# Pooled attention and a multiplicative feed-forward on one core: the last two chunks of 512 tokens by one level of Strassen's scheme

## The chip, the cores and the metric

The kernel runs on one core of a Trainium2 chip. The metric is the device time of one execution in microseconds (us). Before the change three runs took 415.0, 415.41 and 415.67 us; the median is 415.41. One execution was also taken by the profiler.

Names of engines in the profile: PE is the matrix unit (PEld its weight loads), DVE the vector engine, ACT the scalar engine, POOL GpSimd, SP the engine that issues most DMAs. A queue is marked with a q, as in SPq.

## What is computed

Shapes: q, k, v are 8 x 8 x 1152 x 64 (batch, heads, sequence, head size) in fp32; 4608 tokens of 512 come out.

```python
q_pool = q.reshape(B, H, S // 2, 2, D).mean(axis=3)
attn = softmax(q_pool @ k.T / sqrt(D))              # 576 x 1152 for each batch and head
x = (attn @ v).transpose(0, 2, 1, 3).reshape(4608, 512)
h = ((x @ w1) * (x @ w2)) @ w3                      # w1, w2: 512 x 1024, w3: 1024 x 1024
out = h @ w_out                                     # w_out: 1024 x 512
```

## The kernel before, in words

Two heads of one batch are a pair; there are 32 pairs. For each pair the scores, transposed, come off PE in steps of 512 columns for both heads (`scores`, L422), ACT takes the exponential into a large ring of f16 in SBUF (`ring`, L436), and PE multiplies the ring's columns with v (`av_mm`, L449). A unit of this product is 128 pooled tokens of one pair, or 64 of two; there are 144. DVE normalizes (`av_norm`, L479) and the result goes, transposed, to `xT` (512 features on partitions, 4 blocks of 128; 5 x 576 tokens of room). For the first pairs and for the units of 64, PE turns it and DVE copies it (L515, L517), for the others SP's DMA does (`x_dma`, L469).

The feed-forward part works on chunks of 512 tokens, numbers 0 to 8 (`moe_groups`, L582). `T` (`T16`, 1024 x 512 in f16) is w3 times w_out and is made once, early in the run, in groups of eight 256-column matmuls (L544). Per chunk there are 16 projection groups of four 512-column matmuls, w1 and w2 in turn (`proj`, L563, L566): the first result is copied to SBUF as `asb`, the second is multiplied with it into `gT` (gate, L599). Then four groups of eight 512-column matmuls with T (L610) give 128 tokens of output each; they are scaled, copied to `osb` and stored.

A planner (`_visits`, L191) fixes in advance, with costs of its own, in which visit which attention unit and which feed-forward group stands in PE's queue. A chunk is put in the list `loose` under the unit after which its x is there. PSUM has eight banks: one for the product with v and the turns (`avb`), one for groups (`mo`), and three pairs for scores and groups (`psc`, named `mot` for groups). Each engine works through its instructions in the order in which they are written; `manual_schedule` leaves that order alone.

When all units are done (`tail[0]`, L806) only feed-forward groups are left. Then ACT copies `asb` (L593) and shares the scaling (L616 DVE, L617 ACT), and the stores go through SP instead of POOL's queue (L618; L621 before). The last group is cut in 384 and 128 columns (`go_last`, L623) and the last two stores go through ACT's queue. In between, a flag is worked out from the softmax sums: DVE compares (L816 to L824), one small matmul sums over the partitions (L827), and all engines load the flag (L833). If it were set, a slower general path would run behind (`_general`, L24); with these inputs it is not.

POOL casts and adds inputs (`cast_kq`, `cast_v`), issues the early loads, and issues the stores of all chunks but the last ones. SP issues the later loads, the transposes of k and q (L363) and of x (L473).

Of the kernel before, what the change touches and what calls it, by code (L numbers as in the profile page):

```python
# [253 lines left out]

@with_exitstack
def kernel(
# [26 lines left out]
    QM = 4  # L283
# [16 lines left out]
    ps = fast.enter_context(tc.tile_pool(name="ps", bufs=1, space=bass.MemoryType.PSUM))  # L300
# [12 lines left out]
    wosb = msb.tile([128, NF, dm], FP16)  # L313
# [207 lines left out]

    def bank(scored):
        if tail[0] or scored:
            return ps.tile([128, 2, 512], FP32, tag="psc", bufs=3, name="mot")[:, 0, :]
        return ps.tile([128, 512], FP32, tag="mo", bufs=1, name="mo")
# [43 lines left out]
    def store(eng, pos, osb):  # L569
        b, r = pos // (2 * Sq) * 2, pos % (2 * Sq)  # L570
        if r == QM * 128:
            for u in range(2):
                r0 = (b + u) * Sq + QM * 128
                eng.dma_start(out=out[r0:r0 + QT, :], in_=osb[u * QT:u * QT + QT, :])
            return
        if r > QM * 128:
            b, r = b + 1, r - QM * 128 - 2 * QT
        eng.dma_start(out=out[b * Sq:b * Sq + QM * 128, :].rearrange("(p c) n -> p c n", c=QM)[:, r // 128, :], in_=osb)  # L578

    final, near = [], [False]  # L580

    def moe_groups(c):  # L582
# [20 lines left out]
        tts = list(range(0, CH, 128))  # L603
        if c in final:
            tts.sort(key=lambda tt: (c * CH + tt) % (2 * Sq) != QM * 128)
        for n, tt in enumerate(tts):
            def go(po, tt=tt, n=n):
                near[0] = c in final and n >= len(tts) - 3
                for ft in range(NF):
                    nc.tensor.matmul(po, t["g"][:, ft, tt:tt + 128], T16[:, ft, :],  # L610
                                     start=(ft == 0), stop=(ft == NF - 1))

            def put(po, tt=tt):
                osb = msb.tile([128, dm], FP32, tag="osb", bufs=3)
                if tail[0]:
                    nc.vector.tensor_scalar_mul(out=osb[:, 0:256], in0=po[:, 0:256], scalar1=1.0 / (SCL * SCL))  # L616
                    nc.scalar.mul(out=osb[:, 256:512], in_=po[:, 256:512], mul=1.0 / (SCL * SCL))  # L617
                    store(nc.scalar if c in final and tt == tts[-2] else nc.sync, c * CH + tt, osb)  # L618
                else:
                    nc.vector.tensor_scalar_mul(out=osb, in0=po, scalar1=1.0 / (SCL * SCL))  # L620
                    store(nc.gpsimd, c * CH + tt, osb)  # L621

            def go_last(po, tt=tt):  # L623
                osb = msb.tile([128, dm], FP32, tag="osb", bufs=3)
                for hs in (slice(0, 384), slice(384, dm)):
                    ph = ps.tile([128, 2, 512], FP32, tag="psc", bufs=3, name="mol")[:, 0, 0:hs.stop - hs.start]
                    for ft in range(NF):
                        nc.tensor.matmul(ph, t["g"][:, ft, tt:tt + 128], T16[:, ft, hs],
                                         start=(ft == 0), stop=(ft == NF - 1))
                    if hs.start:  # L630
                        nc.scalar.mul(out=osb[:, hs], in_=ph, mul=1.0 / (SCL * SCL))
                    else:
                        nc.vector.tensor_scalar_mul(out=osb[:, hs], in0=ph, scalar1=1.0 / (SCL * SCL))
                store(nc.scalar, c * CH + tt, osb)

            if c in final and n == len(tts) - 1:
                yield 2, go_last, None, 0.0
            else:
                yield 2, go, put, 0.0
# [83 lines left out]
    for c in range(B * Sq // CH):  # L723
        n = 0
        for b in range(B):
            for t in range(NT5):
                if xpos(b, t) < (c + 1) * CH and xpos(b, t) + (128 if t < QM else QT) > c * CH:
                    p = b * HP + HP - 1
                    i = unit_of(p, t)
                    n = max(n, i + 2, index[(p, QM - 1)] + 1 + HELD if p >= XD and t < QM else 0)  # L730
        loose.setdefault(min(n, NU + 1), []).append(c)
    final.extend(loose[max(loose)])
# [40 lines left out]
    for vis in range(NVIS):  # L773
        if vis == T_START:
            queue.append(t_groups())
        for s in range(vis * VS, vis * VS + VS):
            pn = (s * G + G - 1) // FLAT
            if pn != seen:
# [6 lines left out]
                if 0 < pn < NP - 2:  # L785
                    prepare(pn + 2)
                elif pn + 2 == NP:
                    cast_v(NP - 1)
            scores(s)
# [21 lines left out]
    release()  # L811

# [12 lines left out]
    for _ in range(12):  # L825
        fill()
    nc.tensor.matmul(avb[0:1, 0:1], okh, ones, start=True, stop=True)  # L827
    badi = const.tile([1, 1], mybir.dt.int32)
    nc.vector.tensor_scalar(out=badi, in0=avb[0:1, 0:1], scalar1=-1.0, scalar2=float(128 * NQ),
                            op0=ALU.mult, op1=ALU.add)  # L830
    while not near[0]:
        fill()
    bad = nc.values_load(badi[0:1, 0:1], min_val=0, max_val=128 * NQ)  # L833
    while fill():
        pass
    fast.close()
# [32 lines left out]
```

## Time and profile before

| | |
|---|---|
| median of 3 runs | 415.41 us |
| span of the profiled execution, first to last instruction (the profile gives no other time of it) | 414.1 us |
| PE busy, from 328 to 358, 358 to 368, 367.5 to 388.2 and 388.2 to 409.4 us | 30.00, 10.00, 20.70, 21.14 us |
| DVE busy in the same stretches | 17.35, 6.09, 7.28, 7.64 us |
| ACT busy in the same stretches | 19.11, 0.38, 6.21, 6.20 us |
| POOL busy in the same stretches | 3.06, 1.09, 0, 0 us |
| mean granted clock of PE | 0.999 |
| last exponential ends | 349.08 us |
| last matmul ends, last store is issued | 409.34 us, 409.69 us |

How to read the rows of the profile. The page's strips cut the span in 40 equal slices and give the busy share of each in tenths. A row of a group names line, engine, operation, output and inputs with shapes and types, the count, then busy time and mean duration, then the idle time before it and what ended it. A row of the timeline has start, duration, engine, line, operation, and in brackets the idle time before it. In the chain of waits each piece is what the end of the run was waiting for at that time.

### The profile page before, as it was taken

The numbers are of one execution on the slowest core, as the hardware profiler recorded it, in microseconds if no ns is written. First come the engines' busy times: TensorE is split into PE (matmuls) and PEld (weight loads), VectorE is DVE, ScalarE is ACT, GpSimd is POOL, SyncE is SP. The second block draws the span as 40 slices with busy tenths as digits, with TensorE's granted clock in tenths as the row PEclk, the third lists the DMA queues.
The fourth block names the chain that finished last, engine by engine and source line by source line (L and its number), as shares of the span: only waits on it lengthen the run. The fifth ranks groups of instructions, "written<-read, shape, count | busy, mean of one in ns | idle before, by whom it ended". The sixth has DMA issues, their size and how long they took to land.

```text
span 414.1 us, 12744 instructions
## 1 busy us (share of the span) xinstructions
PE 399.9 (97%) x5337; PEld 246.9 (60%) x5337; DVE 205.5 (50%) x573; ACT 323.4 (78%) x353; POOL 167.6 (40%) x212
## 2 busy tenths in 40 slices
PE   3899999999999999999999999999999999999995
PEld 1477787565556655566556556655777655644442
DVE  1256665665356535554455436553556346744241
ACT  4878979898989998899999999999899986022321
POOL 4979976470655316504535155505532210010000
PEclk9999999999999999999999999999999999999999
DMA  8999999999799898959999999998975440030302
GB/s 263 210 320 289 269 286 312 348 247 265 185 238 252 221 286 278 242 70 278 273 264 280 264 252 270 292 260 163 303 207 121 85 90 15 16 114 2 101 0 108
DMA packets 90832, 86.34 MB, mean 209 GB/s; under 512 B 59664, under 2 KB 64272, under 8 KB 90768
## 3 DMA queue, kind: packets, MB, share of 16 engines
q1 hardware_dynamic: 81312, 58.80, 59.1%
q0 software_dynamic: 8880, 25.63, 21.6%
q10 hardware_dynamic: 576, 1.05, 0.8%
q8 instruction: 42, 0.69, 0.7%
q14 instruction: 22, 0.18, 0.1%
HBM read 67.11 MB, written 9.44 MB: 185 GB/s over the span
## 4 chain that ended last, share of the span: by engine, by line
PE 93%; ACT 2%; DMA 2%; DVE 1%; issue 1%; SPq 0%; POOL 0%; ACTq 0%
PE psc L431 20%; PE avb L462 17%; PE mot L566 16%; PE mo L566 15%; PE mo L610 11%; PE mot L610 5%; PE mo L544 3%; PE avb L459 3%; ACT ring L436 2%; PE ptk L371 2%; DMA kst<-in_k_dram 2%; DVE kqT L373 1%; PE mot L544 1%; PE mo L535 1%; PE mot L535 1%
## 5 line engine op out<-in xcount | busy, mean ns | idle before, releaser
L436 ACT ACTIVATE ring<-psc 128x1024 f16<-128x1024 f32 x324 | 308.3, 1025 | 33.8 <-PE psc L431 32.0
L462 PEld LDWEIGHTS <-ring 128*128 128x128 f16 x2304 | 84.4, 98 | 26.3 <-issue 7.1
L431 PE MATMUL psc<-kqT 64*128 64x512 f16 (+7 forms) x1152 | 96.2, 291 | 3.4 <-ACT ring L436 0.9
L462 PE MATMUL avb<-vaug,ring 128*128 128x65 f16 x2304 | 91.4, 193 | 0.0
L343 POOL CAST kq<-kst 128x1152 f16<-128x1152 f32 x31 | 35.7, 1150 | 74.3 <-DMA kqT<-kq 52.3
L431 PEld LDWEIGHTS <-kqT 64*128 64x128 f16 x1152 | 46.0, 95 | 31.0 <-issue 8.4
L578 POOL DMA_DIRECT2D out_dram<-osb x23 | 12.7, 551 | 101.6 <-DVE rzall L483 99.9
L610 PE MATMUL mo<-T,gT 128*128 128x512 f16 x192 | 45.6, 380 | 0.0
L566 PEld LDWEIGHTS <-w2sb 128*128 128x128 f16 x320 | 28.2, 98 | 28.3 <-issue 4.2
L566 PEld LDWEIGHTS <-w1sb 128*128 128x128 f16 x320 | 28.2, 98 | 27.7 <-issue 3.9
L610 PEld LDWEIGHTS <-gT 128*128 128x128 f16 x280 | 25.3, 98 | 32.2 <-issue 5.2
L483 DVE RECIPROCAL rzall<-avb 128x2 f32<-128x2 f32 x144 | 23.8, 165 | 37.0 <-PE avb L462 20.2
L566 PE MATMUL mot<-xT,w1sb 128*128 128x512 f16 (+2 forms) x172 | 41.1, 364 | 0.1
L620 DVE TENSOR_SCALAR osb<-mo 128x512 f32<-128x512 f32 x24 | 16.6, 692 | 48.5 <-PE mo L610 48.5
L347 POOL TENSOR_TENSOR kq<-qst 128x512 f16<-128x512 f32 x31 | 39.4, 1272 | 1.2 <-DMA qst<-in_q_dram 1.2
L566 PE MATMUL mot<-xT,w2sb 128*128 128x512 f16 (+2 forms) x156 | 38.0, 368 | 0.0
L356 POOL CAST vaug<-vst 128x1152 f16<-128x1152 f32 x32 | 36.6, 1143 | 2.6 <-DMA vst<-in_v_dram 2.5
L599 DVE TENSOR_TENSOR gT<-mot,asb 128x512 f16<-128x512 f32 x37 | 25.6, 692 | 22.0 <-PE mot L566 20.8
L599 DVE TENSOR_TENSOR gT<-mo,asb 128x512 f16<-128x512 f32 x35 | 24.2, 692 | 24.6 <-PE mo L566 24.4
L566 PE MATMUL mo<-xT,w2sb 128*128 128x512 f16 (+2 forms) x164 | 36.2, 349 | 0.0
L595 DVE COPY asb<-mo 128x512 f32<-128x512 f32 x32 | 22.1, 691 | 24.0 <-PE mo L566 23.7
L566 PE MATMUL mo<-xT,w1sb 128*128 128x512 f16 (+2 forms) x148 | 33.1, 351 | 0.0
(76 smaller groups left out, 287.4 us busy)
## 6 DMA issues: line engine op xcount, KB each, us to landing
vst<-in_v_dram SPq DMA_DIRECT2D x25, 576.0 KB, 4.9
kst<-in_k_dram SPq DMA_DIRECT2D x23, 576.0 KB, 5.9
qst<-in_q_dram SPq DMA_DIRECT2D x23, 512.0 KB, 7.2
out_dram<-osb POOLq DMA_DIRECT2D x23, 256.0 KB, 5.2
kst<-in_k_dram POOLq DMA_DIRECT2D x8, 576.0 KB, 9.8
qst<-in_q_dram POOLq DMA_DIRECT2D x8, 512.0 KB, 10.4
vst<-in_v_dram POOLq DMA_DIRECT2D x7, 576.0 KB, 7.2
w3c<-in_moe_w_dram POOLq DMA_DIRECT2D x4, 512.0 KB, 8.1
```

Source lines behind the costliest of these rows:

```text
L343: nc.gpsimd.tensor_copy(out=kq16[:, 0:NJ].rearrange("p c u d -> p u c d"), in_=kst.rearrange("p u (c d) -> p u c d", d=D))
L347: eng.tensor_tensor(out=kq16[:, NJ:NJ + QM].rearrange("p c u d -> p u c d"), in0=qv[:, :, :, 0], in1=qv[:, :, :, 1], op=ALU.add)
L356: nc.gpsimd.tensor_copy(out=va[:, :, :, 0:D], in_=vs.pop(p).rearrange("p u (c d) -> p u c d", d=D))
L431: nc.tensor.matmul(psc[:, u, f - s * G:f - s * G + ln], kT2[u * 64:u * 64 + 64, jt, :], qpT[u * 64:u * 64 + 64, i0:i0 + ln], start=True, s ...
L436: nc.scalar.activation(out=ring[:, :, r0:r0 + G], in_=psc, func=AF.Exp, bias=0.0, scale=SCALE)
L462: nc.tensor.matmul(avb[:, o + u * E1:o + u * E1 + E1], ring[:, u, c0:c0 + 128], va[:, u, jt, :], start=(jt == 0 and u == 0), stop=(jt == N ...
L483: nc.vector.reciprocal(out=rzall[:, i, :], in_=av[:, :, D:E1].rearrange("p u o -> p (u o)"))
L566: nc.tensor.matmul(pw[:, d0:d0 + n], wt[:, mc, ft * 128:ft * 128 + 128], xT[:, mc, a:a + n], start=(mc == 0 and d0 == 0), stop=(mc == NC - ...
L595: nc.vector.tensor_copy(out=t["a"], in_=pa)
L599: nc.vector.tensor_tensor(out=t["g"][:, ft, :], in0=pb, in1=t["a"], op=ALU.mult)
L610: nc.tensor.matmul(po, t["g"][:, ft, tt:tt + 128], T16[:, ft, :], start=(ft == 0), stop=(ft == NF - 1))
L620: nc.vector.tensor_scalar_mul(out=osb, in0=po, scalar1=1.0 / (SCL * SCL))
```

## The change

Chunks 7 and 8 leave the list of groups. They are computed behind all other work by `late_chunks`, with one level of Strassen's scheme in Winograd's form. A product of two matrices, each cut in 2 x 2 blocks, is made of seven block products instead of eight; sums of blocks are needed on both sides ahead and of results behind.

There are eight projection sets (`g`: four pairs of 128-feature rows in each half, for w1 and w2) and four output sets (`o`). Each set has seven units, and a unit is four matmuls of 256 columns. POOL makes the sums of weights and T (`weight_sums`, called when the last v has been cast) and of x (`x_sums`, behind the last unit), with four sums for each. Product 1 is copied by ACT into a second bank, on which product 2 accumulates; products 6, 7 and 4 accumulate in the first bank, with a copy by ACT in between; products 5 and 3 accumulate in a third bank. ACT takes products out of PSUM, DVE adds the last two combinations from PSUM and SBUF. Where w2 is used the results are multiplied with those of w1: from PSUM by DVE, and those two that come as sums by POOL (even j) or DVE (odd j), which then also makes the four sums of g that the output sets need. The results stand in `room`, which takes the place of the ring.

The order of the 84 units and their banks comes from a second planner, `_Late`, which also has costs of its own. The pool of PSUM tiles is closed after the last unit and the eight banks become tiles of their own (`banks`); the last groups of chunk 6 use three of them. The stores of chunks 5 and 6 go through SP, not POOL. The flag's matmul is written right before the first unit and its load before the last six units. `go_last` is gone; the last chunk's first-half rows are stored in halves of 256 columns.

```diff
+class _Late:
...
+    UNIT = 0.436
+    SEEN = {"act": 0.25, "dve": 0.25, "pool": 0.25}
+    AFTER = {1: (), 5: (), 6: (1,), 2: (1,), 7: (6,), 4: (7,), 3: (7, 5)}
...
+    @staticmethod
+    def order(sets, full, width=300, look=3):
...
-    ps = fast.enter_context(tc.tile_pool(name="ps", bufs=1, space=bass.MemoryType.PSUM))
+    banks8 = fast.enter_context(ExitStack())
+    ps = banks8.enter_context(tc.tile_pool(name="ps", bufs=1, space=bass.MemoryType.PSUM))
...
-    wosb = msb.tile([128, NF, dm], FP16)
+    wosb = msb.tile([128, NF, dm], FP16, tag="wo", bufs=1, name="wosb")
...
+    banks, turns = [], [0]
+
     def bank(scored):
-        if tail[0] or scored:
+        if tail[0]:
+            turns[0] += 1
+            return banks[turns[0] % 3]
+        if scored:
             return ps.tile([128, 2, 512], FP32, tag="psc", bufs=3, name="mot")[:, 0, :]
         return ps.tile([128, 512], FP32, tag="mo", bufs=1, name="mo")
...
-                    store(nc.scalar if c in final and tt == tts[-2] else nc.sync, c * CH + tt, osb)
-                    store(nc.gpsimd, c * CH + tt, osb)
...
+                store(nc.sync if c >= LATE - 2 else nc.gpsimd, c * CH + tt, osb)
...
+    HF, HM, HC = NF // 2, dm // 2, CH // 2
+    LATE = B * Sq // CH - 2
+    IS = 1.0 / (SCL * SCL)
+    wS, tS, xS = [], {}, {}
+    def minus(out, x, y):
+        nc.gpsimd.tensor_tensor(out=out, in0=x, in1=y, op=ALU.subtract)
+    def weight_sums():
+        for w, tag in ((w1sb, "kst"), (w2sb, "vst")):
+            st = [att.tile([128, 2, NC // 2, dff // 2], FP16, tag=tag, name="wS") for _ in range(2)]
+            a11, a12 = w[:, 0:NC // 2, 0:dff // 2], w[:, NC // 2:NC, 0:dff // 2]
+            a21, a22 = w[:, 0:NC // 2, dff // 2:dff], w[:, NC // 2:NC, dff // 2:dff]
+            s1, s2, s3, s4 = st[0][:, 0], st[0][:, 1], st[1][:, 0], st[1][:, 1]
+            nc.gpsimd.tensor_tensor(out=s1, in0=a21, in1=a22, op=ALU.add)
+            minus(s2, s1, a11)
+            minus(s3, a11, a21)
+            minus(s4, a12, s2)
+            wS.append({1: a11, 2: a12, 3: s4, 4: a22, 5: s1, 6: s2, 7: s3})
+        b11, b12 = T16[:, 0:HF, 0:HM], T16[:, 0:HF, HM:dm]
+        b21, b22 = T16[:, HF:NF, 0:HM], T16[:, HF:NF, HM:dm]
+        st = [att.tile([128, 2, HF, HM], FP16, tag="qst", name="tS") for _ in range(2)]
+        t1, t2, t3, t4 = st[0][:, 0], st[0][:, 1], st[1][:, 0], st[1][:, 1]
+        minus(t1, b12, b11)
+        minus(t2, b22, t1)
+        minus(t3, b22, b12)
+        minus(t4, b21, t2)
+        tS.update({1: b11, 2: b21, 3: b22, 4: t4, 5: t1, 6: t2, 7: t3})
+    def x_sums():
+        st = msb.tile([128, 2, 4, NC // 2, HC], FP16, tag="wo", bufs=1, name="xS")
+        for c in (0, 1):
+            (_, a, n), = runs(LATE + c)
+            b11, b12 = xT[:, 0:NC // 2, a:a + HC], xT[:, 0:NC // 2, a + HC:a + n]
+            b21, b22 = xT[:, NC // 2:NC, a:a + HC], xT[:, NC // 2:NC, a + HC:a + n]
+            x1, x2, x3, x4 = (st[:, c, i] for i in range(4))
+            minus(x1, b12, b11)
+            minus(x2, b22, x1)
+            minus(x3, b22, b12)
+            minus(x4, b21, x2)
+            xS[c] = {1: b11, 2: b21, 3: b22, 4: x4, 5: x1, 6: x2, 7: x3}
+    def late_chunks(before_end):
+        room = att.tile([128, 27, 512], FP32, tag="ring", bufs=1, name="room")
+        halves = room.bitcast(FP16)
+        sets = [("g", j, w) for j in range(4) for w in range(2)] + [("o", c, u) for c in range(2) for u in range(2)]
+        order, bank = _Late.order(sets, {n % 3 for n in range(1, turns[0] + 1)})
+        gs = [msb.tile([128, NF, CH], FP16, tag="g8", bufs=2, name="gT") for _ in range(2)]
+        sg = [halves[:, 19 + 4 * c:23 + 4 * c, :].rearrange("p n (f i) -> p n f i", f=HF) for c in range(2)]
+        spare, held, at, done = list(range(19)), {}, {}, set()
...
+        def unit(k, p):
+            if k[0] == "g":
+                c, j = divmod(k[1], 2)
+                a, b = wS[k[2]][p], xS[c][p]
+                left = [a[:, :, (2 * j + f) * 128:(2 * j + f) * 128 + 128] for f in range(2)]
+                n, kc = HC, NC // 2
+            else:
+                c, u = k[1:]
+                g = gs[c]
+                a = {1: g[:, 0:HF, 0:HC], 2: g[:, HF:NF, 0:HC], 4: g[:, HF:NF, HC:CH],
+                     5: sg[c][:, 0], 6: sg[c][:, 1], 7: sg[c][:, 2], 3: sg[c][:, 3]}[p]
+                b = tS[p]
+                left = [a[:, :, u * 128:u * 128 + 128]]
+                n, kc = HM, HF
+            pt = banks[bank[k, {1: "x", 6: "x", 7: "x", 4: "x", 2: "y", 5: "z", 3: "z"}[p]]]
+            for f, l in enumerate(left):
+                for i in range(kc):
+                    nc.tensor.matmul(pt[:, n * f:n * f + n], l[:, i, :], b[:, i, :],
+                                     start=(p in (1, 5) and f == 0 and i == 0), stop=(i == kc - 1), skip_group_check=True)
+            return pt
...
+        def stored(k, c):
+            i = int(c[1]) - 1
+            done.add((k, c))
+            pos = (LATE + k[1]) * CH + i * HC + k[2] * 128
+            row = at[k, "row", i]
+            if k[1] == 1 and i == 0:
+                n = int(c[2]) - 1
+                store((nc.sync, nc.scalar)[k[2]] if n else nc.sync, pos, row[:, n * HM:n * HM + HM],
+                      slice(n * HM, n * HM + HM))
+            elif {(k, c[:2] + "1"), (k, c[:2] + "2")} <= done:
+                store(nc.sync, pos, row)
+                drop((k, "row", i))
+        def step(k, p):
+            pt = unit(k, p)
+            a = ("g", k[1], 0)
+            gated = k[0] == "g" and k[2] == 1
+            last = k[1] % 2
+            side = nc.vector if last else nc.gpsimd
+            w = CH if k[0] == "g" else HM
+            def whole(c):
+                i, n = int(c[1]) - 1, int(c[2]) - 1
+                if gated:
+                    nc.vector.tensor_tensor(out=part(k[1] // 2, last, i, n), in0=flat(pt), in1=flat(at[a, c]), op=ALU.mult)
+                    drop((a, c))
+                elif k[0] == "g":
+                    nc.scalar.copy(out=slot((k, c)), in_=pt)
+                else:
+                    nc.scalar.mul(out=out_part(k, c), in_=pt[:, 0:HM], mul=IS)
+                    stored(k, c)
+            def plus(c, pz, u):
+                i, n = int(c[1]) - 1, int(c[2]) - 1
+                if k[0] == "o":
+                    nc.vector.scalar_tensor_tensor(out=out_part(k, c), in0=pz[:, 0:HM], scalar=IS, in1=at[k, u][:, 0:HM],
+                                                   op0=ALU.mult, op1=ALU.add)
+                    drop((k, u))
+                    stored(k, c)
+                    return
+                nc.vector.tensor_tensor(out=slot((k, c)), in0=pz, in1=at[k, u], op=ALU.add)
+                drop((k, u))
+                if gated:
+                    side.tensor_tensor(out=part(k[1] // 2, last, i, n), in0=flat(at[k, c]), in1=flat(at[a, c]), op=ALU.mult)
+                    drop((k, c))
+                    drop((a, c))
+            def keep(u):
+                if k[0] == "g":
+                    nc.scalar.copy(out=slot((k, u)), in_=pt)
+                else:
+                    nc.scalar.mul(out=slot((k, u))[:, 0:HM], in_=pt[:, 0:HM], mul=IS)
+            if p == 1:
+                nc.scalar.copy(out=banks[bank[k, "y"]][:, 0:w], in_=pt[:, 0:w])
+            elif p == 6:
+                keep("u2")
+            elif p == 7:
+                keep("u3")
+            elif p == 2:
+                whole("c11")
+            elif p == 4:
+                whole("c21")
+            elif p == 3:
+                plus("c12", pt, "u2")
+            done.add((k, p))
+            if p in (7, 5) and {(k, 7), (k, 5)} <= done:
+                plus("c22", banks[bank[k, "z"]], "u3")
+            if gated and all((k, q) in done for q in _Late.AFTER):
+                c = k[1] // 2
+                s1, s2, s3, s4 = (sg[c][:, n, 2 * last:2 * last + 2] for n in range(4))
+                g11, g21, g12, g22 = (part(c, last, i, n) for n in range(2) for i in range(2))
+                for o, x, y, op in ((s1, g12, g22, ALU.add), (s3, g11, g12, ALU.subtract),
+                                    (s2, s1, g11, ALU.subtract), (s4, g21, s2, ALU.subtract)):
+                    side.tensor_tensor(out=o, in0=x, in1=y, op=op)
+        for n, (k, p) in enumerate(order):
+            if n == len(order) - 6:
+                before_end()
+            step(k, p)
...
-        loose.setdefault(min(n, NU + 1), []).append(c)
-    final.extend(loose[max(loose)])
+        if c < LATE:
+            loose.setdefault(min(n, NU + 1), []).append(c)
...
+                    weight_sums()
...
+    x_sums()
+    banks8.close()
+    lp = banks8.enter_context(tc.tile_pool(name="lp", bufs=8, space=bass.MemoryType.PSUM))
+    banks.extend(lp.tile([128, 512], FP32, tag="b", name=f"b{i}") for i in range(8))
...
-    for _ in range(12):
-        fill()
-    nc.tensor.matmul(avb[0:1, 0:1], okh, ones, start=True, stop=True)
-    badi = const.tile([1, 1], mybir.dt.int32)
-    nc.vector.tensor_scalar(out=badi, in0=avb[0:1, 0:1], scalar1=-1.0, scalar2=float(128 * NQ),
-                            op0=ALU.mult, op1=ALU.add)
-    while not near[0]:
-        fill()
-    bad = nc.values_load(badi[0:1, 0:1], min_val=0, max_val=128 * NQ)
     while fill():
         pass
+    nc.tensor.matmul(banks[7][0:1, 0:1], okh, ones, start=True, stop=True)
+    badi = const.tile([1, 1], mybir.dt.int32)
+    nc.vector.tensor_scalar(out=badi, in0=banks[7][0:1, 0:1], scalar1=-1.0, scalar2=float(128 * NQ),
+                            op0=ALU.mult, op1=ALU.add)
+    bads = []
+    late_chunks(lambda: bads.append(nc.values_load(badi[0:1, 0:1], min_val=0, max_val=128 * NQ)))
+    bad, = bads
```

## The prediction

> **What bounds the kernel now.** I read the page first, then the chain of waits in order of time for the end of the run, then that end's timeline, and the stages of the last 90 us.
>
> ```profile
> span 414.1 us, 12744 instructions
> PE 399.9 (97%) x5337; PEld 246.9 (60%) x5337; DVE 205.5 (50%) x573; ACT 323.4 (78%) x353; POOL 167.6 (40%) x212
> PE   3899999999999999999999999999999999999995
> ACT  4878979898989998899999999999899986022321
> POOL 4979976470655316504535155505532210010000
> PEclk9999999999999999999999999999999999999999
> ```
>
> PE is busy 97% of the span, at full clock in all slices. ACT and POOL fall to a quarter or nothing in the last seventh: attention is over there, and PE works alone with light eviction. The chain says which work this is:
>
> ```profile
> 362.50 5.18 PE mot L610 x24
> 367.68 8.63 PE mot L566 x40
> 376.31 0.10 PE avb L827
> 376.41 5.29 PE mot L566 x24
> 381.69 6.91 PE mot L610 x32
> 388.60 13.81 PE mot L566 x64
> 402.42 5.18 PE mot L610 x24
> 407.60 1.76 PE mol L628 x16
> ```
>
> Columns: start, us, what. From 367.68 on the chain is PE without a gap: chunk 7 (64 projection matmuls, 32 with T), then chunk 8. Nothing but the number of streamed columns sets this stretch. So columns taken away there come off the end one for one, unless something else becomes late.
>
> **What is removed.** Chunks 7 and 8 are 8.63+5.29+6.91+13.81+5.18+1.76 = 41.6 us, 192 matmuls of 512 columns (the last 16 are eight, split 384 and 128); 13.81/64 = 0.2158 us each.
>
> **What PE gets instead.** Eight projection sets and four output sets, seven products each: 84 units of 4 matmuls, 336 of 256 columns. The trace has this shape, in the group that makes T (columns: start, us, engine, line):
>
> ```profile
> 65.44 1.04 PE L544 MATMUL mo<-wosb,w3T 128*128 128x256 f16 x8
> 65.38 0.81 PEld L544 LDWEIGHTS <-w3T 128*128 128x128 f16 x8
> ```
>
> Eight take 1.04 us, the last one 0.273 by its group's mean: (1.04-0.273)/7 = 0.1096 us apart, with one weight load each, beside them. 336 x 0.1096 = 36.8 us (36.3 at half the 512-column spacing). **Term: -4.8 us**, at best -5.3. One eighth of the columns is gone, and almost an eighth of the time.
>
> **The change of banks.** PSUM's old pool is closed and eight banks are opened as tiles before the last two T groups of chunk 6. In the changed program's built order the first matmul into a new bank waits for a DVE count, and counting DVE's instructions it is the eviction of the T group just before, though that lies in another bank.
>
> ```profile
> 362.34 3.83 PE L610 MATMUL mot<-T,gT 128*128 128x512 f16 x17
> 364.26 0.69 DVE L620 TENSOR_SCALAR osb<-mot 128x512 f32<-128x512 f32 x1 [1.18 <-PE mot L610]
> ```
>
> Now the next group follows at 362.34 + 8 x 0.2158 = 364.07. With the wait it starts when that eviction is done, 364.95, and a little after: **+0.9 us**, all on the path; PE's whole queue stands behind it. Bounds: 0 if another wait already covered it, 1.1 with a slow release. Work of PE up to there is in the same order in both programs.
>
> **Evictions.** ACT gets per first-weight set five 512-column copies, per second-weight set three, per output set five of 256: 32 x 0.585 (asb<-mot, L593) + 20 x 0.383 (L617) = 26.4 us within 36.8. Twelve of these go from PSUM to PSUM, which no row shows; nearest is the same copy to SBUF, which I take; bounds 0.4 and 0.95 (the 1024-column exponential's 1.025 us, less a little), a loss of 0 to 1 us. DVE gets 24 of 512 columns from PSUM at 0.692 (gT<-mot, L599), four products in SBUF and eight f16 sums in SBUF, eight of 256 (0.425, L616): 16.6 + 2.8 + 8 x s + 3.4. No row has an f16 sum; ok<-ok takes 0.459 for 288 fp32, the 128x512 f16 copy 0.414. I take s = 0.42, by the copy, which is f16 too; 0.69 is the upper end (L599). DVE's sum is 26 to 28 us of 36.8.
>
> [...]
>
> Neither engine is full, but locally DVE is: in units 20 to 65, 46 x 0.438 = 20.1 us, it has 19 x 0.692 + 4 x 0.69 + 4 x 0.42 + 0.43 = 18.0 us, so 2 us of slack. A product that accumulates into a bank ACT still copies waits about 0.2 (PE's end to ACT's start) + 0.585, two units; the written order leaves two to six units between, two or three in the output sets. For close calls of both kinds **+0.4 us**, bounds 0 and 2.
>
> **Pool.** It gets 12 sums of 1024 columns (weights and T), eight of 512 (x), then four products and eight sums of 512 for the even sets. Its rows: kq<-qst 512 columns 1.272 us, the 128-column one 0.450: 2.14 ns a column + 0.18, so 2.4 for 1024, with f16 operands as uncertain as 0.6 to 1.0 of it (operand reads no dearer than fp32). Weight sums: 12 x 2.4 = 28.4 us after the last v cast, which ended at 328.9 and may now come earlier, because the chunk-5 store ahead of it leaves Pool: done by 357.3. That stretch has 3 us of Pool work now. The x sums of chunk 7 wait for the last xT copy (358.05): done by 363.2; those of chunk 8 for the last x transpose, about 366: done by 371. First needed at 369.4 (unit 2) and 379 (unit 24). Cost 0; cover 6 and 8 us; if Pool took 1.7 times as long, every further us would be lost. The later Pool work (15 us) is needed at units 55 and 73, up to 6 us later than I have it.
>
> **Moved and small.** Six stores leave POOL for SP. The first, due near 327.2, now stands ahead of the last k/q transpose, which went at 322.21: that lands near 330 instead, and is first read at 336.3, 6 us of cover. The flag's matmul moves from 376.2 to before the first unit: its DVE chain ends at 366.57, PE comes at 368.4; still 0.1 us. Loading the flag to registers, 0.48 us on PE's sequencer, with 0.7 us of lead at 403.3, now comes six units before the end; 0, bound 0.4. At the end the last eviction is DVE's 256 columns (0.425) instead of ACT's 128 (0.28), +0.15. The last store is half as large, but three others go in the last 1.8 us: 0, bounds -0.4 and +0.5.
>
> **Sum.** -4.8 + 0.9 + 0.4 + 0.15 = -3.35. Span 414.1 - 3.35 = 410.75. The three timed runs are 415.0, 415.41, 415.67, so 0.9 to 1.6 us lie around the span; I leave that unchanged: 415.41 - 3.35 = **412.1 us**.
>
> **The rivals.** First and strongest, on the slower side: **DVE and Pool stand in each other's way**. Twelve new DVE operations read two SBUF tensors, and Pool's twelve do the same. Eight of DVE's (four products, the four sums of the second set) fall while Pool is at work on the even sets. If one had to finish before the other starts, each would lose half to a whole Pool operation: 8 x 0.64 to 1.27 = 5 to 10 us, of which 2 fit into DVE's slack. That costs PE 3 to 8 us; I take 4: 416.1. It decides from 3.35 + 2 = 5.4 us of such waits, 0.67 each. The trace says little. Before now DVE reads two SBUF tensors near Pool only twice, L399 at 4.00 for 0.42 us and 5.22 for 0.43; Pool's next operations start at 4.43 and 5.68, right behind, but their loads had just landed (0.75 + 3.6, 1.28 + 4.3), so it may be chance. Elsewhere Pool's sums take 1259 to 1288 ns beside any DVE work, always DVE with one operand in PSUM.
>
> [...]
>
> Second, **part of the gain is eaten**: s = 0.69, PSUM-to-PSUM copies at 0.75, tighter waits. Losing 0.025 us in each of 84 units is 2.1 us: 414.2. For it, DVE's 2 us of slack; against, ACT's 10 us.
>
> Third, **Pool late**: sums at over 4 us each would delay PE's third unit; at 1.7 times my price for the even sets, unit 73. About 418.
>
> Fourth, **the wait at the change of banks is not there**: 411.2.
>
> **Chances.** Forecast, with the fourth as its edge, 0.55, from 410.8 to 413.5; DVE against Pool 0.25; gain eaten 0.15; Pool late 0.05. Range 411.0 to 416.5: it leaves out some 0.05 below, and above 0.1 of the second case and the 0.05. A measurement here tells about 0.2%, 0.83 us. Faster by more: 0.55 + 0.12 = 0.67. Within: 0.03 + 0.09 = 0.12. Slower: the rest of the collision and Pool late, 0.21.
>
> **What would show it.** After 368.5 a chain of PE alone, 256-column matmuls 0.11 apart, and 37 us later its end; one idle PE interval near 364 released by DVE; DVE's two-input products at 0.7 and sums at 0.42 whatever Pool does. If these stretch to 1.3 or start late, next to Pool's operations, and PE waits for DVE and Pool around 385 to 400, the first rival holds. If the third unit waits for Pool, the Pool estimate is wrong.

## The result, and the profile after

The changed kernel takes 418.91 us (median of 417.17, 418.78, 419.05 and 419.31) against 415.32 for the kernel before in the same series: ratio 1.0078, interval 1.0057 to 1.0100. Forecast were 412.1 us and "faster"; it is slower, and above the range.

The profiled execution took 419.31 us with a span of 417.5. The page's head, in the same columns as before:

```profile
span 417.5 us, 13093 instructions
...
PE 395.7 (95%) x5473; PEld 260.3 (62%) x5473; DVE 219.6 (53%) x593; ACT 335.9 (80%) x381; POOL 213.5 (51%) x237
...
PE   3899999999999999999899999999999999999992
...
PEclk9999999999999999999999999999999999999997
```

PE's busy time fell by 4.2 us (399.9 to 395.7), nearly what the columns promised, yet the span grew by 3.4. So PE waits where it did not, and the last slice says where to look first: PE is busy two tenths of it (before, five). From the kernel before to this profile the difference splits with almost no remainder:

| stretch | before to after, us | forecast |
|---|---|---|
| a wait near 206 us, in code that both kernels share | +1.65 | none |
| first group in the new banks starts 2.67 instead of 1.73 behind the one ahead of it | +0.94 | +0.9 |
| columns (40.49 us from that group to PE's end where nothing waits, x5 below) | -4.8 | -4.8 |
| PE's waits for DVE in the late chunks (42.81 instead of 40.49) | +2.3 | +0.4 |
| last matmul's end to end of span: 4.76 (409.34 to 414.1) to 8.06 (409.48 to 417.54) | +3.3 | +0.15 |

These are the waits of PE after 355 us (columns: who waits, for whom, us in total, times, longest). Before, the same view was empty:

```profile
PE b L851 <- DVE room L902: 1.1, 1, 1.1
PE b L851 <- DVE room L936: 0.8, 1, 0.8
PE b L755 <- DVE osb L764: 0.8, 1, 0.8
```

The last line is the change of banks, the first two lie at 396.46 and 394.80. In the spacing of the matmuls, 0.11 us elsewhere, these two waits cost 1.22 and 1.00 us (the view counts from the end of the last matmul), and a third break at 389.4 costs 0.09: together the 2.3 of the table.

The end in rows, first of the kernel before (ACT's last eviction and store, one store behind PE's end at 409.34), then of the changed kernel (PE's last matmuls, and SP's last four stores, of which two begin behind PE's end at 409.48, as does one of ACT):

```profile
409.38 0.28 ACT L631 ACTIVATE osb<-mol 128x128 f32<-128x128 f32 x1 [0.90 <-PE mol L628]
409.69 0.42 ACTq L578 DMA_DIRECT2D out_dram<-osb  x1
```

```profile
408.44 1.04 PE L851 MATMUL b<-T,room 128*128 128x256 f16 x8
408.87 2.52 SPq L729 DMA_DIRECT2D out_dram<-room  x4
```

And this is the chain of the changed kernel near 206 us (start, us, what):

```profile
197.28 9.00 DMA xT<-xb
206.28 0.04 issue
206.32 0.38 PE mo L717
```

PE's projection waits there for a transposing transfer that SP issued at 197.28. It is absent in the profile of before, and present in this one (1.9 us) and in three of the eleven later profiles (2.1 us in x2, 1.3 in y1, 0.5 in x8), of kernels whose work is the same up to there. Executions of one kernel differ by up to some 5 us, and those of the kernel before do too (14 of its 70 runs beside the later experiments took 416.6 to 421.4 us; none of these has a trace); so below I compare stretches that this wait does not touch, with medians beside them: PE from the first group in the new banks to its last matmul ("PE stretch", 42.81 in the changed kernel), and from there to the end of the span ("end", 8.06).

### The profile page after: what moved, and what is told of

Same layout as the page of the kernel before. It is cut to its first block, busy times and chain, and to the rows that moved or that the text cites. A ratio compares the mean times of both kernels' runs of the same rounds, so it can differ in the third digit from the quotient of the medians.

```text
span 417.5 us, 13093 instructions
## 1 busy us (share of the span) xinstructions
PE 395.7 (95%) x5473; PEld 260.3 (62%) x5473; DVE 219.6 (53%) x593; ACT 335.9 (80%) x381; POOL 213.5 (51%) x237
## 4 chain that ended last, share of the span: by engine, by line
PE 88%; DMA 3%; DVE 3%; ACT 2%; issue 1%; SPq 1%; ACTq 0%
PE psc L577 19%; PE avb L608 16%; PE mo L717 14%; PE mot L717 9%; PE mo L755 9%; PE b L851 8%; PE mo L695 3%; PE avb L605 3%; DMA xT<-xb 2%; ACT ring L582 2%; PE ptk L517 2%; DMA qst<-in_q_dram 1%; DVE room L936 1%; PE b L755 1%; PE mot L755 1%
## 5 line engine op out<-in xcount | busy, mean ns | idle before, releaser
L729 POOL DMA_DIRECT2D out_dram<-osb x18 | 9.9, 552 | 55.5 <-DVE rzall L629 55.5
L755 PEld LDWEIGHTS <-gT 128*128 128x128 f16 x224 | 19.8, 98 | 26.5 <-issue 6.3
L717 PEld LDWEIGHTS <-w2sb 128*128 128x128 f16 x256 | 21.9, 97 | 20.8 <-issue 4.2
L717 PEld LDWEIGHTS <-w1sb 128*128 128x128 f16 x256 | 22.0, 97 | 20.3 <-issue 3.9
L643 DVE TENSOR_TENSOR xb<-avb,rzall 128x128 f16<-128x128 f32 x96 | 28.0, 291 | 3.3
L717 PE MATMUL mot<-xT,w1sb 128*128 128x512 f16 (+1 forms) x108 | 24.7, 355 | 0.1
L717 PE MATMUL mot<-xT,w2sb 128*128 128x512 f16 (+1 forms) x92 | 21.6, 361 | 0.0
```

The lines of the kernel that those rows point to most:

```text
L643: nc.vector.tensor_tensor(out=xbt, in0=av[:, :, 0:D], in1=rzall[:, i, :].unsqueeze(2).to_broadcast([128, 2, D]), op=ALU.mult)
L717: nc.tensor.matmul(pw[:, d0:d0 + n], wt[:, mc, ft * 128:ft * 128 + 128], xT[:, mc, a:a + n], start=(mc == 0 and d0 == 0), stop=(mc == NC - ...
```

## The experiments

**x1, end stores on ACT.** Theory: the end is long because SP, which runs the closing waits, issues stores until the last.

```diff
-                store((nc.sync, nc.scalar)[k[2]] if n else nc.sync, pos, row[:, n * HM:n * HM + HM],
+                store(nc.scalar if n else nc.sync, pos, row[:, n * HM:n * HM + HM],
...
-                store(nc.sync, pos, row)
+                store(nc.scalar if k[1] == 1 else nc.sync, pos, row)
```

> The changed kernel, but the last three stores of the last chunk that SP issued (two of 256 KB, one of 128 KB) are issued by ACT. Theory: in the changed kernel SP is the last to leave the program, since it issues stores until 411.4 us, then has nothing for 2.7 us (414.21, code after the branch being fetched), and only then runs its closing waits, 2.5 us long; with the stores on ACT, SP's pause lies beside the last transfers, and the end is the last landing (413.9) plus 1.8 as before: about 1.8 us less than the changed kernel, 417.1 us. Rival: the last transfers set the end, about 1 MB in the last 4 us; which engine issues them changes nothing: within 0.5 us of 418.9.

Measured: 416.88 us, ratio to before 1.0041 (1.0018 to 1.0065), 2.0 us under the changed kernel by medians. But the PE stretch is 42.81 again and the end 7.60, only 0.46 less; the profile has no wait near 206 us, which would account for the rest of the 2.0; for the other runs that is not shown. From the last landing to the end it took 2.24 instead of 3.67 us, so the pause of SP did leave the path. The last landing came 5.37 instead of 4.38 us after PE's end, though: one store on ACT took 1.96 us to issue (others 0.36), and ACT's next waited behind it. The theory holds for one part of the end; a second part moved with the stores.

**x2, no branch at the end.** The guarded call behind `tc.If(bad > 0)` is removed.

> The changed kernel without the guarded general path at its end: the branch on the count of bad rows and the code behind it are left out. Theory (SP's pause behind the branch lies on the path): the pause of 2.7 us is gone, SP's closing waits begin at 411.5 and stand at the last landing at 413.9; about 1.8 us less than the changed kernel, 417.1 us, and PE's 3.3 us at the branch are gone too. Rival (transfers set the end, the pause is a shadow of it): under 0.5 us less.

Measured: 415.23 us, 0.9986 (0.9965 to 1.0006); PE stretch 42.81, end 5.76: 2.3 us less than the changed kernel in that stretch alone, more than the theory asked. SP's view of waits in the changed kernel names the pause (it stands at the line of the branch and waits for nothing else):

```profile
SPq L1142 <- SPq L1142: 2.7, 1, 2.7
```

Without the branch that line is gone. Another thing went with it. In the changed kernel SP's last store but one took 1.09 us to issue, here three together 1.38 (SP's timeline, first of the changed kernel, then of x2):

```profile
409.80 1.09 SPq L729 DMA_DIRECT2D out_dram<-room  x1
```

```profile
409.16 1.38 SPq L729 DMA_DIRECT2D out_dram<-room  x3
```

In the trace's transfers a fetch of 16 KB on an instruction queue (a fetch of code) begins 0.08 us after PE's last matmul and takes 0.95 us, so it ends at 1.03; SP's long issue begins at 0.32 and ends at 1.41, 0.38 behind it. The same distance, 0.37 to 0.40 us, lies between the fetch's end and that of the long issue in every profile that has both: fetch and issue last 1.55 and 1.68 us (x8), 1.92 and 1.96 (x1), 1.37 and 1.51 (x5), 1.67 and 1.81 (x7), 0.95 and 0.91 (x3). As 0.38 is what an issue takes otherwise, the held one ends as if it began when the fetch is done. Not every issue is held (ACT's store at 0.49 us took 0.36 in the changed kernel). In x2 no such fetch comes before 1.6 us, and the last five issues take 0.34 to 0.41.

The last landing is not earlier in x2, though: it comes 4.67 us after PE's end against 4.38 in the changed kernel. What x2 gains lies behind it: from the last landing to the end it takes 1.09 us instead of 3.67. By this reading the held issue counts in the changed kernel only by the 0.7 us (1.09 - 0.38) by which SP reaches its branch later.

**x4, one PSUM bank kept.** Theory: the 0.94 us at the change of banks are a wait for the eviction just ahead, and a bank outside the closed pool removes it.

```diff
+    kept = fast.enter_context(tc.tile_pool(name="kept", bufs=1, space=bass.MemoryType.PSUM))
-        return ps.tile([128, 512], FP32, tag="mo", bufs=1, name="mo")
+        return kept.tile([128, 512], FP32, tag="mo", bufs=1, name="mo")
...
-        fill(True)
+        fill(avn[0] < NU)
-    banks.extend(lp.tile([128, 512], FP32, tag="b", name=f"b{i}") for i in range(8))
+    banks.extend(lp.tile([128, 512], FP32, tag="b", name=f"b{i}") for i in range(7))
+    banks.append(kept.tile([128, 512], FP32, tag="mo", bufs=1, name="mo"))
```

> The changed kernel, but one PSUM bank stays in a pool of its own through the change of banks, and the last product with T ahead of it writes there. Theory: PE's first group in the new banks no longer waits 0.9 us for DVE's eviction of the group just before it; all later work comes 0.9 us sooner: 418.0 us. Rival: PE's later waits for DVE (0.83 and 1.06 us at 395 to 397.5) grow by what is gained here, since DVE and Pool set the pace there: within 0.3 us of 418.9.

Measured: 417.99 us, 1.0066 (1.0032 to 1.0099). The first group in the new banks starts 1.73 us behind the one ahead (362.07, 363.80), the wait is gone from the view, and the PE stretch behind it is the same (42.82): nothing takes its place. The interval of the medians alone would not show 0.9 us; the stretch does.

**x5, Pool without its late products and sums.** Theory: DVE and Pool stand in each other's way.

```diff
-                if gated:
+                if gated and last:
                     side.tensor_tensor(out=part(k[1] // 2, last, i, n), in0=flat(at[k, c]), in1=flat(at[a, c]), op=ALU.mult)
...
-                    side.tensor_tensor(out=o, in0=x, in1=y, op=op)
+                    if last:
+                        side.tensor_tensor(out=o, in0=x, in1=y, op=op)
```

> The changed kernel without the two products and four sums that Pool does for each of the blocks 0 and 2 in the late chunks; Pool only fills those tiles with ones ahead of them, so a quarter of the late gated values and half of their sums are not computed. Theory (DVE and Pool stand in each other's way): DVE's sums take 0.42 us each throughout instead of 1.2 to 1.37, its products 0.7 instead of 1.29 and 1.45, and PE's two waits of 0.83 and 1.06 us at 395 to 397.5 are gone: 1.9 us less, 417.0 us. Rival: DVE's own load sets these waits: DVE's rows get shorter, the waits stay, and the time is within 0.5 us of 418.9.

Measured: 415.82 us, 1.0004 (0.9973 to 1.0035); PE stretch 40.49, 2.3 us less, no wait of PE left in it; end 8.44. DVE in the changed kernel (timeline: start, us, line, tiles, shapes, count; "room<-b,room" has one operand in PSUM, "gT<-room" and "room<-gT" read SBUF twice):

```profile
383.67 0.69 DVE L902 TENSOR_TENSOR room<-b,room 128x512 f32<-128x512 f32 x1 [1.11 <-PE b L851]
384.40 1.29 DVE L905 TENSOR_TENSOR gT<-room 128x512 f16<-128x512 f32 x1
385.61 1.27 DVE L902 TENSOR_TENSOR room<-b,room 128x512 f32<-128x512 f32 x2
386.92 1.45 DVE L905 TENSOR_TENSOR gT<-room 128x512 f16<-128x512 f32 x1
...
391.88 2.40 DVE L936 TENSOR_TENSOR room<-gT 128x512 f16<-128x512 f16 x2
394.21 1.37 DVE L936 TENSOR_TENSOR room<-room,gT 128x512 f16<-128x512 f16 x1
395.61 1.26 DVE L936 TENSOR_TENSOR room<-gT,room 128x512 f16<-128x512 f16 x1
```

Pool in the same stretch of the same kernel:

```profile
383.99 2.72 POOL L936 TENSOR_TENSOR room<-gT 128x512 f16<-128x512 f16 x2
386.67 1.15 POOL L936 TENSOR_TENSOR room<-room,gT 128x512 f16<-128x512 f16 x1
...
392.79 2.51 POOL L936 TENSOR_TENSOR room<-gT 128x512 f16<-128x512 f16 x2
```

And DVE in x5, the same operations:

```profile
382.55 0.69 DVE L905 TENSOR_TENSOR gT<-room 128x512 f16<-128x512 f32 x1
...
384.67 0.69 DVE L905 TENSOR_TENSOR gT<-room 128x512 f16<-128x512 f32 x1
...
389.80 0.75 DVE L938 TENSOR_TENSOR room<-gT 128x512 f16<-128x512 f16 x2
390.46 0.42 DVE L938 TENSOR_TENSOR room<-room,gT 128x512 f16<-128x512 f16 x1
```

Read the three together: beside Pool a product goes from 0.69 to 1.29 and 1.45, a sum from 0.42 to 1.26 and 1.37, while the operations with one operand in PSUM stay near 0.68 (two in 1.27) with Pool at work all along. Pool's own sums lose less: two in 2.72 or 2.51 us instead of 2.30 (twice 1.15, what a sum of x of this shape takes in the same profile, L775). In all DVE loses 4.8 us here (1.4 on two products, 3.4 on four sums), PE 2.3.

**x3, all of that work on DVE.**

```diff
-            side = nc.vector if last else nc.gpsimd
+            side = nc.vector
```

> The changed kernel with all eight products and sixteen sums of the late blocks' gated values on DVE, none on Pool, in the same order on PE. Theory (the two engines stand in each other's way only while both read two SBUF operands): every product takes 0.69 us and every sum 0.42 us; DVE gets 4 products and 8 sums more (6.1 us) but loses the stretching (4.8 us: products 1.29 and 1.45 to 0.69, sums 5.1 us to 1.7), so its load hardly grows, PE's waits of 0.83 and 1.06 us at 395 to 397.5 shrink to under 0.7 together, and the time is 1.2 to 1.9 us below the changed kernel's (executions without the wait of 1.9 us near 206 us: 417.2 to some 415.6). Rival (DVE's load sets the pace): PE waits for DVE at more places, by 2 us or more in all, and the time is 417.2 or above.

Measured: 416.79 us, 1.0037 (1.0004 to 1.0070); PE stretch 42.17, 0.64 less. Every product takes 0.69 and every sum 0.42, as the theory has it, but PE still waits 1.26 us. In the longer wait (1.05, until 392.06) it stands for a product that DVE does at 391.32, behind a block's four sums (389.85 to 391.40). Both were half right: nothing is stretched any more, but DVE's queue keeps 1.7 of the 2.3 us (42.17 against 40.49).

**x7, products that read PSUM.** The sums that DVE makes for blocks 1 and 3 stay in their PSUM bank. That bank goes on accumulating, so product 3 falls on the kept sum instead of on product 5, and quadrant 12 of these blocks has one addend too many.

```diff
-                nc.vector.tensor_tensor(out=slot((k, c)), in0=pz, in1=at[k, u], op=ALU.add)
+                nc.vector.tensor_tensor(out=pz if own else slot((k, c)), in0=pz, in1=at[k, u], op=ALU.add)
```

> The changed kernel, but the sums that DVE makes for blocks 1 and 3 ahead of their products stay in PSUM, so that these products read one PSUM and one SBUF operand instead of two SBUF operands. Theory (only operations with two SBUF operands are held up by Pool, as DVE's products and sums with a PSUM operand took 0.67 to 0.69 beside Pool too): the two products at 384 and 387 take 0.69 instead of 1.29 and 1.45; DVE is 1.4 us earlier by 388, and PE's waits at 395 to 397.5 shrink, at most by 1.4 us in all: 415.8 to 416.8 in executions without the wait near 206 us. Rival (Pool's work slows DVE whatever it reads, or the sums after it give it back): products stay above 1.2, or the time is within 0.3 us of 417.2.

Measured: 418.69 us, 1.0113 (1.0072 to 1.0153); PE stretch 42.94. DVE in this kernel, with Pool's sums running from 381.42 to 386.0:

```profile
381.84 0.69 DVE L908 TENSOR_TENSOR gT<-b,room 128x512 f16<-128x512 f32 x1
...
383.97 0.69 DVE L908 TENSOR_TENSOR gT<-b,room 128x512 f16<-128x512 f32 x1
```

The mechanism is confirmed at the operand: the same product, beside Pool, 0.69 instead of 1.29 and 1.45. The gain in time did not come: PE's wait of 0.83 falls to 0.43, but its next product into that bank has to wait until DVE has read it (0.46 us), and the four stretched sums, which were left as they were, set the later wait of 1.06.

**x6, stores in halves.** Theory: bunched bytes set the last landing.

```diff
-            if k[1] == 1 and i == 0:
+            if k[1] == 1 or i == 0 and k[2] == 1:
...
-                store((nc.sync, nc.scalar)[k[2]] if n else nc.sync, pos, row[:, n * HM:n * HM + HM],
+                store(nc.scalar if k[1:] == (1, 1) and i != n else nc.sync, pos, row[:, n * HM:n * HM + HM],
```

> The changed kernel with the last chunk's rows and one row of the chunk ahead stored in halves as each half is done, and ACT issuing two of the last four. Theory (transfers bunched at the end): from 408.9 us some 0.64 MB are left instead of 1.0 MB; the last landing comes about 1.0 us after what it was less (4.4 us behind the last matmul to 3.4), and the time is 1.0 us lower: 416.2 in executions without the wait near 206 us. Rival (SP's pause behind the branch and the closing waits set the end whatever the bytes): SP issues as many stores, its pause still begins near 411, and the time is within 0.4 us of 417.2.

Measured: 417.94 us, 1.0053 (1.0019 to 1.0087); end 9.06, the longest of all. The theory fell: fewer bytes were left at PE's end (0.79 MB instead of 1.05), but in more stores, two of which were held (1.66 and 1.24 us) during the fetch of code; the last landing came 6.36 us after PE's end instead of 4.38, and SP reached its branch 1.1 us later. What went up is the number of issues still to come when the fetch starts (four instead of three); the bytes alone do not set this end.

**x8, the changed kernel again.**

> The changed kernel once more, to tell its usual executions from those with PE's wait of 1.9 us near 206 us for a transposing transfer. Theory (that wait belongs to an execution, not to the change, since the work up to there is the same in both kernels): the runs fall in two groups some 1.9 us apart, near 417.2 and 419.1, and the profile of a run of the lower group has no such wait. Rival (the change brings it): all runs lie near 419.

Measured: 419.55 us, 1.0099 (1.0067 to 1.0132); its profile has only 0.5 us of the wait near 206 us, and still a span of 417.9; the six runs lie between 417.52 and 421.16 us and do not fall in two groups. So the theory is not the whole of it. The PE stretch is 44.48 instead of 42.81 with the same waits (1.89 us). Windows of this profile (columns: window and length, busy us of PE, PEld, DVE, ACT, POOL with counts, granted clock, DMA share, GB/s):

```profile
393.00:396.40 3.40, 1.50 (x13) 1.11 (x13) 3.37 (x5) 0.45 (x2) 3.10 (x3) 0.99 0.00 0
396.40:399.80 3.40, 3.40 (x19) 2.40 (x17) 3.04 (x6) 0.74 (x2) 0.00 (x0) 0.50 0.01 2
```

For 3.41 us PE runs at half clock: 19 matmuls instead of some 33, 1.67 us lost. x6 has the same (395.5 to 398.9). The full-clock stretches in the profiles last 375.47, 385.71, 389.12 or 392.53 us, which lie 3.41 us apart, or 10.24, three times that; so in these executions the clock changed on a grid of 3.41 us. Where both waits of PE (0.84 and 1.06) fall into one piece of the grid, PE is busy 1.50 us of it (x8, and x6 from 392.1 to 395.5), and the next is at half clock. x1 has the same waits, placed otherwise:

```profile
391.50:394.90 3.40, 1.83 (x16) 1.26 (x14) 3.37 (x4) 1.35 (x4) 3.32 (x4) 1.00 0.00 0
394.90:398.30 3.40, 3.07 (x29) 2.73 (x29) 3.37 (x7) 1.37 (x4) 0.69 (x1) 1.00 0.01 2
```

There 1.83 us were busy, and the clock stayed, as it did in the changed kernel behind the wait near 206 us (1.74 us busy from 204.65 to 208.06). So whether PE's waits cost 2.3 or 4.0 us (PE stretch 42.81 or 44.48 against 40.49) goes with where an execution lies on this grid. A limit in busy time is not shown: in y1 the last piece with work (405.16 to 408.57) has 1.51 us busy too, and the one behind it is still at full clock.

**x9, the last chunk's product with T as before.** All findings on the end together: fewer, evenly spaced stores, the last one behind the fetch. With it go that chunk's sums.

```diff
-        sets = [("g", j, w) for j in range(4) for w in range(2)] + [("o", c, u) for c in range(2) for u in range(2)]
+        sets = [("g", j, w) for j in range(4) for w in range(2)] + [("o", 0, u) for u in range(2)]
...
-            if gated and all((k, q) in done for q in _Late.AFTER):
+            if gated and k[1] < 2 and all((k, q) in done for q in _Late.AFTER):
...
+        for n, tt in enumerate(tts):
...
+                    nc.tensor.matmul(po[:, hs], gs[1][:, ft, tt:tt + 128], T16[:, ft, hs],
+                                     start=(ft == 0), stop=(ft == NF - 1))
...
+            store(nc.scalar if n > 1 else nc.sync, c * CH + tt, osb)
```

> The changed kernel with the last chunk's product with T made without the scheme: four groups of eight matmuls on 512 columns, evicted in halves by DVE and ACT, and stored one after the other as in the kernel before. Terms, against the changed kernel's usual 417.2: PE 4 groups of 1.73 instead of 14 units of 0.437, +0.8; the end (last matmul to end of span) 4.8 to 5.3 us as before instead of 8.1 to 8.5, -3.2, if bunched stores, a store held by the fetch of code and SP's late pause are what makes it long; the sums of the last chunk go (four of Pool that stood beside DVE's, four of DVE's), so that PE's waits at 395 to 397.5 shrink by 0 to 1.9 us, say -1.0. In all 413.8 us, below the kernel before. Rival (the end is long for another reason, as the eight banks or the many tiles): only the first and last terms, 417.0.

Measured: 413.33 us, 0.9949 (0.9929 to 0.9968), 0.5 us below what was expected. PE stretch 41.98 (0.41 of waits), 0.8 less than the changed kernel's where 0.2 was expected; end 5.14, 2.9 less where 3.2 was expected. The end in its timeline:

```profile
406.00 0.56 DVE L952 TENSOR_SCALAR osb<-b 128x384 f32<-128x384 f32 x1 [0.93 <-PE b L949]
406.38 0.28 ACT L954 ACTIVATE osb<-b 128x128 f32<-128x128 f32 x1 [0.91 <-PE b L949]
406.69 0.35 ACTq L729 DMA_DIRECT2D out_dram<-osb  x1
```

Only one store is left when PE ends (406.35). PE reaches its branch 2.32 us ahead of that end instead of 0.91, the fetch runs from 405.52 to 406.40, the one store near it was issued at 405.51, and none of the last four is held (0.33 to 0.36). The rival, eight banks or many tiles as the cause of the long end, is out: x9 has both.

**y1 and y2, with the bank kept, and then all on DVE.**

> The same with one PSUM bank kept through the change of banks. If the two are independent, another 0.8 us less: 413.0 us. Rival: the 0.8 us is lost again in PE's later waits for DVE: 413.8.

> The same with one PSUM bank kept, and all products and sums of the late blocks on DVE, none on Pool. Theory: with the last chunk's sums gone DVE has room for Pool's part (4 products of 0.69, 4 sums of 0.42: 4.4 us); nothing is stretched, PE's waits there stay under 0.5 us: 412.5. Rival (DVE is the bound of the late chunks): PE waits for DVE by 1 us or more, 414 or above.

Measured: y1 412.37 us, 0.9922 (0.9893 to 0.9951), although its profile has a wait of 1.28 us near 206; PE stretch 41.98 as in x9, the bank's wait gone. y2 412.89, 0.9934 (0.9912 to 0.9957), PE stretch 42.42 with 0.62 of waits. The bank's gain adds to x9's. DVE alone is no better than DVE and Pool: the collisions that x9 left (1.29, 1.45 and one sum of 1.11) fit into slack. y1 is the fastest by its median, below both kernels of the study; x9, y1 and y2 overlap in their intervals.

## Why the prediction was wrong, point by point

- **Columns, -4.8**: right. Where nothing waits (x5) 40.49 us from the first new bank; less two groups with T and the flag (3.64 us in the changed profile, 366.67 to 370.31) leaves 36.85, forecast 36.8.
- **Change of banks, +0.9**: right, 0.94, shown by x4.
- **Close calls, +0.4**: PE lost 2.3 us. The cause is not a close call but the first rival, which the sum put at nothing: it gave DVE's operations with two SBUF operands 0.69 and 0.42 us whatever Pool does, and beside Pool they took 1.29 and 1.45, and 1.2 to 1.37. I described this rival rightly and priced it at 3 to 8, with 4 taken, which was too much; the stated point, from which it alone turns the sign, was 5.4 us of waits on DVE, and DVE's were 4.8. It held, and was not enough by itself: with it and all else as forecast the sum is -4.8 + 0.9 + 2.3 + 0.15 = -1.45, still faster. (The 0.2 us from PE's end to ACT's start was too much as well: the rows of the kernel before have 0.04 to 0.12.)
- **The end, "The last store is half as large, but three others go in the last 1.8 us: 0, bounds -0.4 and +0.5"**: this is the step that failed: +3.3 with the last eviction, instead of +0.15. I looked at the size of the last transfer. What the runs showed in its place is the queue of SP, which runs the closing waits (from 414.21 us on in the changed kernel). In the changed kernel the stores bunch, so SP issues until 1.9 us after PE's end, and one issue is held for 1.09 us by a fetch of code. Then SP reaches its own branch, last of the engines, and stands 2.7 us, until 4.74 us after PE's end; the last landing (4.38) is over by then. In the kernel before, SP was at its branch 1.27 us ahead of PE's end, and its pause lay beside the last store and its landing (2.91); the fetch ran from 0.57 us ahead of PE's end to 0.38 us behind it, and the two issues near it took 0.36 and 0.42 us. x2 takes the fetch and the pause away (-2.3); x9 spaces the stores, so that no issue is held and the pause again lies beside the transfers (-2.9). As x9 changes all of this at once, the shares of bunching, held issue and pause are not separated. What starts the fetch is not shown either: it begins 0.32 to 1.75 us behind PE's branch in the profiles that have one.
- **Flag load, 0**: right for the load; the branch that it serves was not in my sum.
- **Pool, moved stores, 0**: right. No wait of PE for Pool or for a moved store appears in the waits.
- **What no step had**: executions with the wait near 206 us (1.65 in the profiled one) and with a half-clock stretch (1.67 in x8). In the traces of x8 and x6 the second follows on PE's two waits (0.84 and 1.06 us), which the change brought. With them the changed kernel's sums close: -4.8 + 0.94 + 2.3 + 3.3 + 1.65 = 3.4 (417.5 - 414.1), and -4.8 + 0.94 + 2.3 + 1.67 + 3.74 = 3.85 (417.94 - 414.1) for x8.

Why the transfer near 206 us is late in some executions stays open: SP's queue there issues back to back, 2.04 us for a load in the changed kernel that took 0.42 in the kernel before, but x1 shows the same 2.05 without PE waiting. Whether the change makes it more frequent was not settled.

## What to carry to other kernels

Cost the end of a program as a stage of its own: count the stores that are still to be issued when the matrix engine ends, which engine issues the last and which one closes the program, and what a final branch costs (2.3 us of the end here, x2). A scheme that saves columns by adding sums has to place them with the engine beside them in mind: here a DVE operation with two SBUF operands took two to three times as long beside GpSimd (0.69 to 1.29 and 1.45 us, 0.42 to 1.26 and 1.37), one with an operand in PSUM stayed at 0.67 to 0.69. Apply such a scheme only where its outputs have time to leave; here the scheme in five of the six late products (four projections, one with T) and a plain last one gave the gain that the full change lost.

## What the hardware showed unexpectedly

- A store's issue on SP or ACT that met a 16 KB fetch of code took 0.91 to 1.96 us instead of 0.34 to 0.41, and ended 0.37 to 0.40 us after the fetch. Why some issues are not held stays open.
- SP stood 2.7 us behind the branch before its first closing wait (2.5 in the kernel before and in x9, 3.5 in x1); in x2, without branch, there was no such pause.
- Two waits of PE of 0.84 and 1.06 us within one stretch of 3.41 us went with half the granted clock for the next 3.41 us, at a busy time of 1.50 us in both executions; at 1.74 and 1.83 us the clock stayed, and so it did once at 1.51 (y1).
- The first group in a bank of a pool that was just closed waited here for the newest eviction of that pool, from another bank: 0.94 us, and 0 with one bank kept outside.
